# One core, attention and a gated MLP: when the third weight set, a later set's six pieces and the residual x are loaded

## The chip, the cores and the metric

The kernel runs on one core of one Trainium2 chip. The time is that of one execution on the device, in microseconds (us); a result is the median of several runs. A profile is one further execution, recorded instruction by instruction; its span runs from the first to the last instruction on the core.

## The reference

x has 2048 rows of 576. The result is x, plus sliding-window attention (32 heads of 18, window 256) on the normalised x, plus a gated MLP on the normalised x:

```python
def _A_ref(x, wqkv, wo):          # D = 576, H = 32, Dh = 18, W = 256
    qkv = (x @ wqkv).reshape(B, S, 3, H, Dh).transpose(2, 0, 3, 1, 4)
    q, k, v = qkv[0], qkv[1], qkv[2]
    scores = jnp.einsum("bhqd,bhkd->bhqk", q, k) * (Dh ** -0.5)
    mask = (idx[:, None] - idx[None, :] >= 0) & (idx[:, None] - idx[None, :] < W)
    p = _softmax(jnp.where(mask[None, None], scores, -1e9))
    o = jnp.einsum("bhqk,bhkd->bhqd", p, v)
    return o.transpose(0, 2, 1, 3).reshape(B, S, D) @ wo
def _B_ref(x, w1, w3, w2):        # F = 4608
    return (_silu(x @ w1) * (x @ w3)) @ w2
xn = _layernorm(x)
return x + _A_ref(xn, A_wqkv, A_wo) + _B_ref(xn, B_w1, B_w3, B_w2)
```

(The B_x that the inputs hold is not used. Everything is bf16.)

## The kernel before

The program is recorded operation by operation in Python, in the order in which the lines run; `add` notes engine, reads and writes, and `resolve` works out the semaphore waits. So each engine and each DMA queue executes its instructions in the order of the recording, and a DMA that waits holds up every DMA behind it on the same queue. Two queues issue DMAs: SP's, with nearly all of them, and ACT's, with most W2 blocks and some packs.

The 2048 rows go through in four chunks c of 512. A chunk has these stages:

- projection (L437): q, k and v of the chunk from xnT (the normalised x, transposed) and the packed weights wp and wv. In chunk 0 it is part of the start; in the later ones it opens the chunk.
- 36 units u (the loop `for u in range(NF)`): each computes 128 of the 4608 columns of h with 18 matmuls (L664; nine steps n, two matmuls each, on the two halves of the rows of TensorE). Steps 4 to 7 read xnS, a copy of xnT with its two partition halves exchanged. ScalarE takes the tanh (L673), VectorE makes h (L679, L682) into hT. Between the steps stand the score matmuls of the attention (L557) and, three times in a chunk, the P·V matmuls (L614).
- the W2 stage (`p2_list`, `p2_item`): two halves of the output columns, each 9 blocks of W2 by 16 matmuls (L715), and in each half 20 matmuls of the output projection (L721) and four sums with the residual x (L728), each stored by a DMA on SP (L730). `p2_list` numbers its items n from 0: items 0 to 167 are the first half, 168 to 335 the second. The fourth P·V (after item 19) and its transposes lie in here too.

Weights are loaded as they are needed. A set of W1 and W3 columns (w13, one buffer of 128 x 9 x 512) serves four units. It comes in six pieces of 192 KB, each one DMA on SP by `load_part` (L323), always in the order of the sets: set 0 for units 0 to 3 of chunk 0, and so on, nine to a chunk. There are three buffers; set 3 alone goes into a part of hT that is not in use yet. `owed` counts pieces that are due; `owe_part` issues one after steps 3 and 8 of a unit, and the DMA then waits on SP until that matmul is done. So six owed pieces go out over three units. A W2 block (288 KB, four buffers) is loaded by `load_w2` (L350): the first four on SP during units 20 to 26 of chunk 0, all later ones on ACT's queue as soon as the last matmul of the block before in its buffer is done.

The next chunk is prepared meanwhile: its four x tiles come on SP by `load_x` (L299; seven buffers xp), VectorE normalises them (L358 to L370), SP transposes them by DMA (L395) into xnT, and `xn_swap` (L402) makes xnS of it with two DMAs of 256 KB, recorded at an item of the W2 stage. The four tiles of the chunk itself are loaded a second time, for the residual (`xs`).

In chunk 0 the k and q rows are brought into their places by small DMAs from stage (packs, L502): those of groups g 0 and 1 during the projection, the others by `late_spans` at the units listed there, partly on SP, partly on ACT. The packs of the attention's output (L651, `o_pack`) go on SP too. The recording in chunk 0's start is, in the code before:

```python
            if got == ("q", 0):
                load_w13((), 4)
                span_main(0, 2, "act")
                load_w13((), 2)
            elif got == ("q", 2):
                span_last(0, 2)
                for t in (TB, TB + 1):
                    xslot[t] = load_x(t)
```

Set 0 was issued before this; the six pieces here are set 1, and set 2 and set 3 are the twelve pieces that become due at unit 0 (`owed += 12`). From then on a set becomes due after every fourth unit (after unit 15 of chunk 0 none does, since set 3 has freed no buffer of the three); in a later chunk one more becomes due in the projection.

Of the kernel before, what the change touches and what calls it, by code (L numbers as in the profile page):

```python
# [164 lines left out]
def bass_parallel_sum__sliding_block__glu_gated_swiglu__prompt_kernel(  # L165
# [18 lines left out]
    NC = S // CH  # L184
    TB = CH // 128
    G = H // 4
    NF = F // 128
# [10 lines left out]
    with ExitStack() as es:  # L198
# [78 lines left out]
        def job():  # L277
            nonlocal job_ctr
            i = job_ctr % 3
            job_ctr += 1  # L280
            return JOBS[i]
# [13 lines left out]
        def load_x(t, eng="sp"):  # L295
            nonlocal xp_ctr
            s = xp_ctr % NXP
            xp_ctr += 1
            add(eng, lambda e: e.dma_start(xp[s][:], x2[t * 128:(t + 1) * 128, :]), w=[("xp", s)], dma=f"xp{s}")  # L299
            return s  # L300
# [3 lines left out]
        def w13_at(k):  # L304
            if k == 3:
                return NW13, hT[:, 18:27, :]
            s = (k if k < 3 else k - 1) % NW13
            return s, w13[s]

        owed = 0  # L310

        def load_part(after=(), behind=()):

            nonlocal nfill
            if nfill >= 6 * NC * NFC:
                return
            k, i = divmod(nfill, 6)
            s, dst = w13_at(k)
            part, n = divmod(i, 2)
            c0 = (k % NFC) * 512  # L320
            src = (B_w3, B_w1)[n]
            nfill += 1
            add("sp", lambda e: e.dma_start(  # L323
                dst[64 * n:64 * n + 64, 3 * part:3 * part + 3, :],
                src[192 * part:192 * part + 192, c0:c0 + 512].rearrange("(kd p) f -> p kd f", p=64)),
                r=list(behind), after=after, dma=f"w13_{s}_{n}", **{"j" if i else "w": [("w13", s)]})

        def load_w13(behind=(), parts=6):
            for _ in range(parts):
                load_part((), behind)  # L330

        def last_pe():
            return next(o for o in reversed(P.ops) if o.eng == "pe")
# [131 lines left out]
        def proj_end(later=None, late=None):  # L465
            if pend:
                c, what, banks, last = pend.pop()
                proj_part(c, what, banks, 1, last)
                proj_out(c, what, banks, later, late)
                return what  # L470

        def proj_begin(c, what):
            banks = job()
            last = proj_part(c, what, banks, 0)
            got = proj_end()
            pend.append((c, what, banks, last))
            return got
# [256 lines left out]
        xslot = {}  # L734
# [91 lines left out]
        for what in [("q", 0), ("q", 1), ("q", 2), ("q", 3), ("8", 7), None]:  # L826
            got = proj_begin(0, what) if what else proj_end()
# [3 lines that stand above are left out]
                load_w13((), 2)  # L831
            elif got == ("q", 2):
                span_last(0, 2)
                for t in (TB, TB + 1):
                    xslot[t] = load_x(t)

        PV_COST, PV_AFTER = 6.6, 20
        main, rest = span_main, span_last
# [5 lines left out]
        for c in range(NC):  # L844
# [3 lines left out]
            plan = near if c + 1 < NC else {}  # L848
            stat, apply, xt = ({v[k]: i for i, v in plan.items()} for k in range(3))
            loads = {8: (2,), 17: (3,)} if c + 1 < NC else {}  # L850
            total = 9 * NF + len(att) + 3 * PV_COST
            if c:
                total += 9 * sum(COST[kind] for kind, _ in PROJ)
# [59 lines left out]
            for u in range(NF):  # L913
                at_u = u
                if c == 0 and u == 0:
                    owed += 12
                if u in loads:
                    for i in loads[u]:
                        xslot[(c + 1) * TB + i] = load_x((c + 1) * TB + i)
                b0 = jobs[u] = job()  # L920
                for n in range(9):
                    into = nxt - (clock + 9 - n)
                    if done < len(att) and (clock >= nxt or (n == 8 and into < 3 and clock >= soon)):
                        spaced_step()
                    op = unit_pairs(c, u, n, n + 1, b0[0])
                    clock += 1
                    if n in (3, 8):
                        owe_part(op)
                unit_tanh(u, b0[0])
                if u % 4 == 3 and u < NF - 4 and (c or u != 15):  # L930
                    owed += 6
                if next_pv in pv_ready and clock >= pv_ready[next_pv] and next_pv < 3:
                    j = next_pv
                    next_pv += 1
                    banks = job()
                    pv(c, j, banks)
                    clock += PV_COST
                    for g in (2 * j, 2 * j + 1):
                        for s in range(NS):
                            if pt_of[(c, g, s)][0] != "h":  # L940
                                free.append(pt_of[(c, g, s)])
                    later(u, lambda b=banks: (pv_out(b[0], 0), pv_out(b[1], 1), o_scale(0)))
                    later(u + 1, lambda j=j: (o_turn(2 * j, 0), o_turn(2 * j, 1), o_scale(1)))
                    later(u + 2, lambda j=j: o_turn(2 * j + 1, 0))
                    later(u + 3, lambda j=j: (o_turn(2 * j + 1, 1), o_pack(j, "sp")))
                unit_h(u, b0[0])
                for what in side.pop(u, []):
                    what()
                if u in stat:
                    t = (c + 1) * TB + stat[u]  # L950
                    for part in range(2):
                        ln_stats(t, xslot[t], part)
                if u in xt:
                    xn_send((c + 1) * TB + xt[u])
                if u in apply:
                    t = (c + 1) * TB + apply[u]
                    ln_apply(t, xslot[t])
                for span, a, b, n0, n1, eng in late_spans.get(u, []) if c == 0 else []:
                    span(a, b, only=slice(n0, n1), **({"q_eng": eng} if span is main else {"eng": eng}))
                if c == 0 and u in (8, 9, 10, 11):  # L960
                    buf, key = ((wo, "woz"), (oT, "oTz"))[(u - 8) // 2]
                    part = buf[64:128, 4, :] if u % 2 else buf[96:128, 0:4, :]
                    add("dve", lambda e, part=part: e.memset(part.bitcast(dt.float32), 0.0), **{"j" if u % 2 else "w": [key]})
                if c == 0 and u == 13:
                    for t in range(4):
                        rows = A_wo[252 * (t // 2):252 * (t // 2) + 252, :].rearrange("(s p d) f -> p s d f", p=2, d=Dh)[t % 2, :, :, :]
                        add("sp", lambda e, t=t, rows=rows: e.dma_start(wo[0:126, t, :], rows),
                            r=["woz"], dma="wo", **{"j" if t else "w": ["wo"]})
                    add("sp", lambda e: e.dma_start(wo[0:72, 4, :], A_wo[504:576, :]), r=["woz"], j=["wo"], dma="wo")
                if c == 0 and u in (20, 22, 24, 26):  # L970
                    load_w2()
                if u == 29:
                    xs = [load_x(c * TB + tt) for tt in range(TB)]
            assert done == len(att) and next_pv == 3, (done, next_pv)
            ring_of[:] = [*jobs[NF - 2], *jobs[NF - 1]]
# [7 lines left out]
            for n, item in enumerate(p2_list(c)):  # L983
                p2_item(c, item, xs)
                if n == 3:
                    for u in sorted(side):
                        for what in side.pop(u):
                            what()
                elif n == 19:
                    banks = (ring(), ring())  # L990
                    pv(c, 3, banks)
                    pv_out(banks[0], 0)
                    pv_out(banks[1], 1)
                    o_scale(0)
                    o_turn(6, 0)
                    o_turn(6, 1)
                    o_scale(1)
                    o_turn(7, 0)
                    o_turn(7, 1)
                    o_pack(3, "sp")  # L1000
                elif n == 40 and c + 1 < NC:
                    xn_send((c + 1) * TB + 3)
                elif n == 300 and c + 1 < NC:
                    xn_swap(c + 1, ("sp", "sp"))
                elif n in (100, 120) and c + 2 < NC:
                    t = (c + 2) * TB + (n == 120)
                    xslot[t] = load_x(t)

        with nc.Block() as block:
            P.replay(es, block)  # L1010
# [28 lines left out]
```

## Time and profile before

| | |
|---|---|
| time, median of 3 runs | 563.07 us (562.58, 563.07, 564.58) |
| profiled execution | 563.8 us; its span 562.0 us |
| granted clock of TensorE | 1.0 throughout |
| HBM read, written | 71.29 MB, 2.36 MB |
| DMA packets | 126685, 85.83 MB, mean 153 GB/s |

In the profile PE is TensorE's matmuls, PEld its weight loads (beside the matmuls), DVE VectorE, ACT ScalarE, POOL GpSimd; SPq and ACTq are the queues that issue DMAs. A group of instructions goes by its line: L664 the units, L715 the W2 stage, L721 the output projection, L437 the projections. Where the time goes, by stage of chunk 0, from the timeline of TensorE: start and projection to 22.4 us, units to 103.5, W2 stage to 145.3; a later chunk takes 138.1 (145.27 to 283.35). The share of the 16 DMA engines' time that is busy is highest in the first 50 us, where the first sets, wqkv and the packs all go over SP's queue, and around the end of each chunk's units:

```
DMA  9997879887366377588636655859852675470552
```

(one digit for each of 40 slices of the span, in tenths).

### The profile page before, as it was taken

The page shows a single profiled execution, that of the slowest core. Times are in us where ns is not written, and L with a number is a line of the kernel's source. Part 1 is how long each engine was busy: PE and PEld are TensorE (multiplying, and loading weights), DVE is VectorE, ACT ScalarE, POOL GpSimd, SP SyncE. Part 2 cuts the span into 40 slices and gives each one's busy share as a digit, 9 for nine tenths or more (in the row PEclk, how much of TensorE's full clock was granted, in tenths as well). Part 3 has the DMA queues.
Part 4 walks back from the last instruction along what each step waited for, and adds up shares of the span by engine and source line. Part 5 has one row for each costly group of instructions (what it writes and reads, how often), then busy time and mean ns, then how long its engine had stood idle before and what let it go on. Part 6 is the DMA issues. An engine that isn't in the chain of part 4 may idle for free.

```text
span 562.0 us, 15709 instructions
## 1 busy us (share of the span) xinstructions
PE 555.4 (99%) x6765; PEld 343.9 (61%) x6765; DVE 314.9 (56%) x586; ACT 253.0 (45%) x349; POOL 163.3 (29%) x384
## 2 busy tenths in 40 slices
PE   8999999999999999999999999999999999999998
PEld 3545455677676555477767645547776654555776
DVE  7468788810366778861046678884114567767211
ACT  4347766200176766600038676660004766666000
POOL 6413444400033445430003444533000333433000
PEclk9999999999999999999999999999999999999999
DMA  9997879887366377588636655859852675470552
GB/s 245 208 186 170 204 174 176 203 208 187 99 141 135 101 178 144 136 205 203 176 81 139 158 120 131 163 158 201 191 149 64 138 171 127 117 162 12 138 148 64
DMA packets 126685, 85.83 MB, mean 153 GB/s; under 512 B 34024, under 2 KB 124320, under 8 KB 126616
## 3 DMA queue, kind: packets, MB, share of 16 engines
q1 hardware_dynamic: 89076, 63.16, 49.9%
q10 hardware_dynamic: 37540, 21.66, 15.0%
q8 instruction: 53, 0.87, 0.7%
q14 instruction: 16, 0.13, 0.1%
HBM read 71.29 MB, written 2.36 MB: 131 GB/s over the span
## 4 chain that ended last, share of the span: by engine, by line
PE 97%; DMA 2%; DVE 1%; issue 0%; POOL 0%; ACT 0%
PE ps L664 50%; PE ps L715 24%; PE ps L437 9%; PE ps L557 6%; PE ps L614 4%; PE ps L721 3%; DMA w<-in_B_w_dram 1%; DMA xp<-in_A_x_dram 1%; DVE xn L370 0%; DVE stats L358 0%; DVE stats L360 0%; ACT xnT L389 0%; PE ps L382 0%; POOL rstd L364 0%; DVE ofin L728 0%
## 5 line engine op out<-in xcount | busy, mean ns | idle before, releaser
L664 PE MATMUL ps<-xnT,w 64*128 64x512 bf16 x1400 | 181.3, 376 | 1.1 <-issue 1.1
L664 PE MATMUL ps<-xnS,w 64*128 64x512 bf16 x1120 | 154.0, 376 | 0.0
L715 PE MATMUL ps<-w,hT 128*128 128x288 bf16 x1152 | 147.3, 286 | 0.2 <-DMA w<-in_B_w_dram 0.2
L679 DVE SCALAR_TENSOR_TENSOR gs<-th,ps 128x512 bf16<-128x512 bf16 x144 | 98.0, 681 | 78.6 <-ACT th L673 77.5
L566 ACT ACTIVATE pt<-ps 128x1024 bf16<-128x1024 f32 (+1 forms) x112 | 113.1, 1010 | 63.4 <-PE ps L557 63.1
L715 PEld LDWEIGHTS ps<-w,hT 128*128 128x128 bf16 x1152 | 111.9, 98 | 30.8 <-issue 1.7
L664 PEld LDWEIGHTS ps<-xnT,w 64*128 64x128 bf16 x1400 | 70.0, 94 | 59.5 <-issue 1.5
L593 POOL TENSOR_TENSOR pt<-pt,mk 128x128 int32<-128x128 int32 (+1 forms) x199 | 80.4, 425 | 79.4 <-ACT pt L566 79.4
L682 DVE SCALAR_TENSOR_TENSOR hT<-gs,ps 128x512 bf16<-128x512 bf16 x144 | 98.9, 687 | 4.9
L673 ACT ACTIVATE th<-ps 128x512 bf16<-128x512 f32 x144 | 85.5, 593 | 24.0 <-PE ps L664 23.7
L664 PEld LDWEIGHTS ps<-xnS,w 64*128 64x128 bf16 x1120 | 57.2, 94 | 52.4
L728 DVE TENSOR_TENSOR ofin<-ps,xp 128x288 bf16<-128x288 f32 x32 | 14.7, 458 | 120.1 <-PE ps L721 120.1
L450 ACT ACTIVATE stage<-ps 128x512 bf16<-128x512 f32 x16 | 9.6, 597 | 146.0 <-PE ps L437 143.7
L593 POOL TENSOR_TENSOR hT<-hT,mk 128x128 int32<-128x128 int32 (+1 forms) x31 | 12.4, 421 | 171.5 <-ACT hT L566 171.5
L557 PE MATMUL ps<-qv,kv 64*128 64x320 bf16 (+4 forms) x528 | 52.7, 260 | 0.0
L557 PEld LDWEIGHTS ps<-qv,kv 64*128 64x128 bf16 x528 | 27.3, 94 | 25.8 <-ACT pt L566 0.3
L437 PE MATMUL ps<-xnT,wp 64*128 64x512 bf16 (+1 forms) x360 | 38.7, 355 | 0.0
L566 ACT ACTIVATE stage<-ps 128x1024 bf16<-128x1024 f32 x24 | 24.6, 1023 | 12.6 <-PE ps L557 12.6
L636 DVE STREAM_TRANSPOSE od<-oq 128x256 bf16<-128x256 bf16 x64 | 25.8, 428 | 6.3 <-POOL oq L629 6.3
L437 PEld LDWEIGHTS ps<-xnT,wp 64*128 64x128 bf16 x360 | 19.0, 94 | 14.1 <-issue 0.7
L721 PE MATMUL ps<-wo,oT 128*128 128x288 bf16 x160 | 24.8, 286 | 0.0
L593 POOL TENSOR_TENSOR stage<-stage,mk 128x128 int32<-128x128 int32 (+1 forms) x42 | 17.0, 423 | 17.3 <-ACT stage L566 17.2
(58 smaller groups left out, 341.7 us busy)
## 6 DMA issues: line engine op xcount, KB each, us to landing
w<-in_B_w_dram SPq DMA_DIRECT2D x210, 192.0 KB, 4.2
w<-in_B_w_dram ACTq DMA_DIRECT2D x68, 288.0 KB, 3.3
xp<-in_A_x_dram SPq DMA_DIRECT2D x29, 144.0 KB, 4.4
out_dram<-ofin SPq DMA_DIRECT2D x32, 72.0 KB, 1.7
xnS<-xnT SPq DMA_DIRECT2D x8, 256.0 KB, 5.0
oT<-od SPq DMA_DIRECT2D x56, 36.0 KB
pt<-in_A_wqkv_dram SPq DMA_DIRECT2D x4, 288.0 KB, 6.7
hT<-in_B_w_dram SPq DMA_DIRECT2D x6, 192.0 KB, 5.3
```

The lines of the kernel that those rows point to most:

```text
L437: op = add("pe", lambda e, out_=out_, st=st, mv=mv, n=n, r0=r0, first=first: e.matmul(out_, st, mv, start=first, stop=(part == 1 and n == ...
L557: add("pe", lambda e, r0=r0, out_=out_, kb=kb, q0=q0, nb=nb: e.matmul(out_, kb4[r0:r0 + 64, g, kb + NV - NB, :] if kb < 0 else kv[r0:r0 + ...
L566: add("act", lambda e: e.activation(pt_slot(sl)[:, 0:w, :], PS[:, SC[0]:SC[1] + 1, 0:w].rearrange("p r q -> p q r"), ACT.Exp, scale=scale) ...
L593: add("pool", lambda e, vb=vb, mm=mm: e.tensor_tensor(vb, vb, mm, ALU.mult), r=(key if n == 0 else []) + ["mk"], **{"w" if n == 0 else "j" ...
L614: add("pe", lambda e, p=p, q=q, pr=pr, sl=sl, g=g, pos=pos, q0=q0, nb=nb, col=col, first=first, n=n: e.matmul(PS[32 * q:32 * q + VW, banks ...
L636: add("dve", lambda e: e.transpose(od[i][:, g % 2, c0:c0 + CH // 2], oq[:, c0:c0 + CH // 2]), r=["oq", "oq0"], **{"j" if half or g % 2 els ...
L664: op = add("pe", lambda e, n=n, r0=r0, r=r, k=k, src=src: e.matmul(PS[:, b0 + r, :], wt[r0:r0 + 64, k, fl * 128:(fl + 1) * 128], src, star ...
L673: add("act", lambda e: e.activation(th[i][:], PS[:, bg, :], ACT.Tanh, scale=0.5), r=[("ps", bg)], w=[("th", i)])
L679: add("dve", lambda e: e.scalar_tensor_tensor(out=gs[i][:], in0=th[i][:], scalar=1.0, in1=PS[:, bg, :], op0=ALU.add, op1=ALU.mult), r=[("t ...
L682: add("dve", lambda e: e.scalar_tensor_tensor(out=hT[:, u, :], in0=gs[i][:], scalar=0.5, in1=PS[:, bu, :], op0=ALU.mult, op1=ALU.mult), r= ...
L715: add("pe", lambda e: e.matmul(bank, hT[:, f, tt * 128:(tt + 1) * 128], w2[sl][:, k, :], start=(f == 0), stop=False), r=[("h", f), ("w2", ...
L721: add("pe", lambda e: e.matmul(bank, oT[:, k, tt * 128:(tt + 1) * 128], wo[:, k, d0:d0 + HD], start=False, stop=(k == 4)), r=[("oT", j) fo ...
```

## The change

Five edits in the scheduling; no computing instruction changes, and every byte that was loaded is loaded once as before.

- Chunk 0's set 2 is recorded as one run of six pieces right after the packs of groups 0 and 1, where the x tiles 4 and 5 stood. At unit 0 six pieces become due (set 3), not twelve.
- The x tiles 4 to 7 are loaded at units 11, 13, 15 and 17 of chunk 0. Tiles 6 and 7 were at units 8 and 17.
- The set that became due after unit 31 (the second of the next chunk) no longer does; its six pieces are issued in the W2 stage at items 60, 105, 150, 200, 245 and 290, each waiting for the matmul recorded last.
- The residual x tiles are loaded at unit 31, not 29.
- The swap that makes the next chunk's xnS is recorded at item 176, not 300.

```diff
             elif got == ("q", 2):
                 span_last(0, 2)
-                for t in (TB, TB + 1):
-                    xslot[t] = load_x(t)
+                load_w13()
...
             loads = {8: (2,), 17: (3,)} if c + 1 < NC else {}
+            if c == 0:
+                loads = {11: (0,), 13: (1,), 15: (2,), 17: (3,)}
...
                 if c == 0 and u == 0:
-                    owed += 12
+                    owed += 6
...
-                if u % 4 == 3 and u < NF - 4 and (c or u != 15):
+                if u % 4 == 3 and u < NF - 8 and (c or u != 15):
                     owed += 6
...
-                if u == 29:
+                if u == 31:
                     xs = [load_x(c * TB + tt) for tt in range(TB)]
...
-                elif n == 300 and c + 1 < NC:
+                elif n == 176 and c + 1 < NC:
                     xn_swap(c + 1, ("sp", "sp"))
                 elif n in (100, 120) and c + 2 < NC:
                     t = (c + 2) * TB + (n == 120)
                     xslot[t] = load_x(t)
+                elif n in (60, 105, 150, 200, 245, 290) and c + 1 < NC:
+                    load_part((last_pe(),))
```

On TensorE, VectorE, ScalarE and GpSimd the instructions and their order stay the same; only the order of the DMAs on SP changes.

## The prediction

> **What bounds the kernel now.** I read the page first: the share of each engine and the chain of work that ended last.
>
> ```profile
> PE 555.4 (99%) x6765; PEld 343.9 (61%) x6765; DVE 314.9 (56%) x586; ACT 253.0 (45%) x349; POOL 163.3 (29%) x384
> ...
> PE 97%; DMA 2%; DVE 1%; issue 0%; POOL 0%; ACT 0%
> ```
>
> TensorE is busy 555.4 of 562.0 us and holds 97% of the chain. So a change that leaves its instructions as they are can only take away holes in TensorE's stream or make new ones. The waits of PE list all holes:
>
> ```profile
> PE ps L748 <- DVE oq L743: 1.2, 1, 1.2
> PE ps L382 <- DVE xn L370: 1.1, 2, 0.7
> PE ps L664 <- issue: 1.1, 1, 1.1
> PE ps L715 <- DMA w<-in_B_w_dram: 0.2, 1, 0.2
> PE ps L437 <- ACT xnT L389: 0.2, 1, 0.2
> ```
>
> The first, second and last lie before 12.2 us, in the start that the diff does not touch. Two are within its reach: 1.1 at L664 and 0.2 at L715. The timeline of PE shows the first (start, length, engine, line, tiles, count, idle before):
>
> ```profile
> 38.12 0.38 PE L664 MATMUL ps<-xnT,w 64*128 64x512 bf16 x2
> 39.57 1.04 PE L664 MATMUL ps<-xnT,w 64*128 64x512 bf16 x8 [1.06 <-issue]
> ```
>
> The x2 closes unit 7 (its n = 8), the x8 opens unit 8, the first that reads the third weight set, in w13 buffer 2. "issue" means that the profile shows no releaser, so I looked at the queue that loads the set (timeline of SP):
>
> ```profile
> 24.44 0.94 SPq L299 DMA_DIRECT2D xp<-in_A_x_dram  x2
> 25.43 2.78 SPq L323 DMA_DIRECT2D w<-in_B_w_dram  x4
> 28.25 4.66 SPq L502 DMA_DIRECT2D kv<-stage  x3
> 32.95 3.04 SPq L323 DMA_DIRECT2D w<-in_B_w_dram  x2
> 36.03 4.32 SPq L323 DMA_DIRECT2D hT<-in_B_w_dram  x6
> ```
>
> and at the two late pieces alone (L323, issued 32.9 to 36):
>
> ```profile
> L323 SPq DMA_DIRECT2D w<-in_B_w_dram x2: 1466/1496/1527, 33.0 to 34.5; - x2
> ...
>   PEld ps L664: 1.5, 1
> ...
> DMA to landing us min/median/max: 5.0/5.2/5.4
> ```
>
> The last piece goes out at 34.5 and lands 5.0 later, at 39.5; TensorE goes on at 39.57. That hole is the lateness of the third set, which stood behind two x tiles and three packs. The other hole:
>
> ```profile
> 107.06 9.48 PE L715 MATMUL ps<-w,hT 128*128 128x288 bf16 x76
> 116.75 4.58 PE L715 MATMUL ps<-w,hT 128*128 128x288 bf16 x36 [0.21 <-DMA w<-in_B_w_dram]
> ```
>
> A W2 block issued on ACT's queue at 110.69 came late; the chain has 6.00 us of DMA there.
>
> **The change, part by part.** *Third set in one run.* It removes the hole at unit 8. Idle is counted from the end of a matmul, but pairs follow each other every 0.216 us (1.73 for 8 pairs in the chain), so without the wait unit 8 would have begun at 38.12 + 0.216 = 38.34: the loss is 1.23. With the change the six pieces start at 24.44, where the x tiles stood. At 0.70 each (2.78 / 4) the last goes out at about 27.9; the four issued there before took 6.1 to 7.3 us to land, so the set is in by 35.2, 3.1 us before it is read. Gain 1.23.
>
> What is pushed back: four pieces of the fourth set now also precede the packs of g 2 to 4, which move from 28.25 to about 24.44 + 6 x 0.70 + 4 x 0.72 = 31.5 and end near 36.2. Their first reader is the ninth score step, at 51.78. The last two pieces of the fourth set follow by 37.6 and land by 43.6 (6.0, the longest of that set's six); unit 12 needs them at 48.35 - 1.23 = 47.1. The fifth set's last pieces go out near 44.5, before at 51.3 to 52.7; unit 16 reads it at 58.29 - 1.23. The x tiles, now at units 11 and 13 in place of 24.44, go out after 50; DVE first reads one at 71.20 (L358). The moved waits on PE positions name matmuls long done when SP reaches them. All this costs nothing; without that cover each late set would cost about what unit 8 lost.
>
> *Six pieces taken from units 32 to 34 and spread over W2.* Before, they went out from 102.1 to 108.0, beside the first W2 blocks: those issued at 108.7 and 112.7 took 5.3 and 4.9 us, that of 110.69 the 6.00 above. Blocks issued 114.6 to 120.9 took 3.0 to 4.2. A block is wanted three blocks (48 matmuls x 0.1225, 5.88) after its slot came free, about 5.7 after its issue. With the pieces gone, the third block is in time. Last matmul start 116.25, next due 116.38, came at 116.75: gain 0.37. The other chunks show no such hole.
>
> Their new places cost something. Items 60 and 105 go out near 118 to 120, behind the o packs, beside blocks that take 3.0 to 4.2 of 5.7 or more: room 1.5, a piece needs 0.82 (six issued at 158.6 to 162.0 landed after 3.5 to 4.2, so (162.0 + 4.2 - 158.6 - 3.5) / 5). Items 245 and 290 stand beside blocks of 2.9 to 3.4: covered. Items 150 and 200 stand on both sides of the xnS swap, and there is little room:
>
> ```profile
> 126.21 1.19 SPq L402 DMA_DIRECT2D xnS<-xnT  x2
> ```
>
> The swap has the same place: in SP's order it followed the first four stores at once, without a PE wait, so moving it from item 300 to 176 only keeps it ahead of the pieces. But the W2 block issued on ACT right behind it was already nearly late (L350, issued 127.2, and in the third chunk 403.3):
>
> ```profile
> L350 ACTq DMA_DIRECT2D w<-in_B_w_dram x1: 374/374/374, 127.2 to 127.2; - x1
> ...
> DMA to landing us min/median/max: 5.5/5.5/5.5
> ```
>
> ```profile
> L350 ACTq DMA_DIRECT2D w<-in_B_w_dram x1: 375/375/375, 403.3 to 403.3; - x1
> ...
> DMA to landing us min/median/max: 5.6/5.6/5.6
> ```
>
> In the second chunk the same block (265.3) took 4.5. Wanted at 5.68 after issue, less 0.09 between a landing and the matmul (39.48 to 39.57), they have 0.10, -0.02 (call it 0) and 1.10 of room. Item 200 comes at 125.09 + 32 x 0.1225 = 129.0, while the swap still runs (its halves took 4.7 and 5.3 from 126.2 and 126.8). No row has swap, piece and block together, so I bound it: the piece may be served after the block (delay 0), or wholly within its time (0.82); with item 150 having pushed the swap as well, 1.64. With 0 nothing is lost; with 0.82, 0.72 + 0.82 + 0 = 1.54; with 1.64, 1.54 + 1.64 + 0.54 = 3.72. The one comparable row, the swap's own effect, varies by 1.1 us between chunks, so it picks no end; I take half a piece, 0.41: 0.31 + 0.41 + 0 = 0.72. It cannot go below nothing, since the removed pieces never stood beside this block.
>
> The Trainium skill (DMA: Bandwidth & Descriptors, "Queues, rings and completion order") says that each DMA engine takes turns between the queues it has work for, a packet at a time. By that rule SP's piece is served in full while ACT's block is, and the give-back would be that of 0.82, not of 0.41.
>
> *Residual x from unit 29 to 31.* Four issues, now behind four o packs; used only by the first store, some 20 us later. Nothing.
>
> **Sum.** The profiled run took 563.8 (span 562.0 and 1.8 around it): 563.8 - 1.23 - 0.37 + 0.72 = 562.92. It stands 0.73 above the median 563.07, so against the median: 562.19.
>
> **Rivals.**
> 1. *Nothing is given back:* the piece of item 200 waits out the swap on SP's own queue while ACT's block finishes. For it: the block lands only 0.7 after the swap's second half. 563.07 - 1.60 = 561.47.
> 2. *Whole piece inside the block's time:* queues share evenly and the piece is ready 3 us before the block is due. 561.47 + 1.54 = 563.01, no change. The Trainium skill's rule above would bring this one about; the slower block beside the early pieces (5.3 against 3.0) speaks for it, the second chunk's 4.5 beside a swap against so full a price.
> 3. *Slower:* items 150 and 200 both come ahead of the block behind the swap, in all three chunks. It decides against the change once the delay passes 0.85, where the stalls reach 1.60. At 1.64: 561.47 + 3.72 = 565.19. Against it: item 150 goes out near 124, over two us before the swap, when the queues are less full (DMA share 0.80 in 120 to 130).
> 4. *The hole stays or moves to the fourth set:* only if the run of six, with four more behind it, fills the queue so that landings stretch from 7.3 to over 10. 562.19 + 1.23 = 563.42.
>
> **How the numbers follow.** Forecast (part of a piece, 561.7 to 562.7) 0.42; rival 1, 0.30; rival 2, 0.15; rival 3, 0.08; rival 4, 0.05. Time 562.2. The range of 8 in 10 takes in rivals 1 and 2 with some 0.3 of spread between measurements: 561.2 to 563.3. About 0.5%, 2.8 us, is what a measurement of this kernel can tell from no change. Every case above lies within it; faster by so much would need 2.8 us of holes where 1.6 are within reach (0.03), slower needs rival 3 at nearly twice its bound or a new hole in each chunk (0.04), so within 0.5%: 0.93.
>
> **What will show it.** Right: no hole before unit 8; six pieces in a row from about 24.4 on SP; PE 1.2 us earlier from there; no hole at L715 near 115; at most small holes at L715 near 131.5 and 407, released by a W2 block that took 5.7 to 6.3. Wrong: a hole at unit 8 or 12; blocks behind the swap still at 5.5 or less (rival 1), or over 6.5 (rival 3); a DMA wait anywhere at L437 or L557.

## The result and the profile after

The change makes the kernel slower: 565.77 us median (565.05 to 566.75, five runs) against 563.07 (562.58 to 564.58) before, a ratio of 1.0048 with an interval of 1.0034 to 1.0063. The forecast was 562.2, with a range to 563.3. Run once more later (below), the change took 566.07.

The page after: engines, chain, and the waits of PE.

```profile
PE 557.4 (99%) x6765; PEld 344.1 (61%) x6765; DVE 314.6 (56%) x586; ACT 253.0 (45%) x349; POOL 163.2 (29%) x384
...
PE 96%; DMA 3%; DVE 0%; POOL 0%; ACT 0%; issue 0%
```

```profile
PE ps L715 <- DMA w<-in_B_w_dram: 1.7, 3, 0.9
PE ps L748 <- DVE oq L743: 1.2, 1, 1.2
PE ps L382 <- DVE xn L370: 0.6, 1, 0.6
PE ps L437 <- ACT xnT L389: 0.2, 1, 0.2
```

The wait at L664 is gone, as forecast. In its place L715 waits three times for W2 blocks, 1.7 us, where it waited once for 0.2. The first part is plain in the queue and in the units (timeline of SP; the six pieces of the run alone; timeline of PE, where this profile's unit 0 begins at 23.41):

```profile
24.50 4.94 SPq L323 DMA_DIRECT2D w<-in_B_w_dram  x6
29.48 2.58 SPq L323 DMA_DIRECT2D hT<-in_B_w_dram  x4
32.11 3.30 SPq L502 DMA_DIRECT2D kv<-stage  x3
```

```profile
L323 SPq DMA_DIRECT2D w<-in_B_w_dram x6: 612/704/1201, 24.5 to 28.8; - x6
...
DMA to landing us min/median/max: 4.5/4.8/5.0
```

```profile
39.17 1.24 PE L664 MATMUL ps<-xnT,w 64*128 64x512 bf16 x10
40.25 0.35 PE L557 MATMUL ps<-qv,kv 64*128 64x320 bf16 x4
40.44 1.03 PE L664 MATMUL ps<-xnS,w 64*128 64x512 bf16 x8
```

The last piece goes out at 28.8 and is in by 33.8; the x10 at 39.17 holds the end of unit 7 and the first steps of unit 8, with nothing between. The new holes, in the timeline of PE:

```profile
132.82 1.40 PE L715 MATMUL ps<-w,hT 128*128 128x288 bf16 x10 [0.35 <-DMA w<-in_B_w_dram]
```

```profile
269.67 2.13 PE L715 MATMUL ps<-w,hT 128*128 128x288 bf16 x16 [0.40 <-DMA w<-in_B_w_dram]
272.74 3.48 PE L715 MATMUL ps<-w,hT 128*128 128x288 bf16 x27 [0.94 <-DMA w<-in_B_w_dram]
```

They stand in the second half of the W2 stages of chunks 0 and 1, behind the swap. The prediction had looked for small ones near 131.5 and 407; the two in chunk 1 came where it expected none. Chunk 1's queue on SP, before and then after, shows what is new ahead of them:

```profile
256.23 1.06 SPq L299 DMA_DIRECT2D xp<-in_A_x_dram  x2
260.55 3.64 SPq L730 DMA_DIRECT2D out_dram<-ofin  x4
264.29 1.18 SPq L402 DMA_DIRECT2D xnS<-xnT  x2
```

```profile
256.28 0.69 SPq L323 DMA_DIRECT2D w<-in_B_w_dram  x1
257.02 0.60 SPq L299 DMA_DIRECT2D xp<-in_A_x_dram  x1
257.67 0.65 SPq L323 DMA_DIRECT2D w<-in_B_w_dram  x1
258.37 0.59 SPq L299 DMA_DIRECT2D xp<-in_A_x_dram  x1
260.60 1.44 SPq L730 DMA_DIRECT2D out_dram<-ofin  x2
262.09 0.60 SPq L323 DMA_DIRECT2D w<-in_B_w_dram  x1
262.81 1.43 SPq L730 DMA_DIRECT2D out_dram<-ofin  x2
264.35 1.17 SPq L402 DMA_DIRECT2D xnS<-xnT  x2
267.46 13.31 SPq L323 DMA_DIRECT2D w<-in_B_w_dram  x3
```

The first two pieces (items 60 and 105) go out with the two x tiles, before the stores. What they do can be read from the four stores behind them, which are small: before, and after,

```profile
L730 SPq DMA_DIRECT2D out_dram<-ofin x4: 332/334/343, 260.5 to 263.9; - x4
...
DMA to landing us min/median/max: 1.6/2.1/3.0
```

```profile
L730 SPq DMA_DIRECT2D out_dram<-ofin x4: 333/342/528, 260.6 to 263.9; - x4
...
DMA to landing us min/median/max: 5.1/5.9/6.5
```

A store that landed after 2.1 us takes 5.9: when the swap is issued, transfers issued earlier are still waiting to be served, a backlog. The W2 block behind the swap, before and after, takes 7.3 us in place of 4.5:

```profile
L350 ACTq DMA_DIRECT2D w<-in_B_w_dram x1: 375/375/375, 265.3 to 265.3; - x1
...
DMA to landing us min/median/max: 4.5/4.5/4.5
```

```profile
L350 ACTq DMA_DIRECT2D w<-in_B_w_dram x1: 374/374/374, 265.4 to 265.4; - x1
...
  PE ps L715: 0.9, 1
...
DMA to landing us min/median/max: 7.3/7.3/7.3
```

It is the block that the hole of 0.94 waits for. The busy share of the DMA engines says the same (windows: busy time of PE, PEld, DVE, ACT, POOL, clock, DMA share, GB/s), before and after:

```profile
256.00:264.00 8.00, 8.00 (x67) 6.40 (x66) 1.83 (x4) 0.00 (x0) 0.00 (x0) 1.00 0.79 200
264.00:272.00 8.00, 8.00 (x68) 6.37 (x67) 0.00 (x0) 0.00 (x0) 0.00 (x0) 1.00 0.89 221
```

```profile
256.50:265.50 9.00, 9.00 (x76) 7.20 (x74) 1.83 (x4) 0.00 (x0) 0.00 (x0) 1.00 1.05 246
265.50:273.50 8.00, 6.66 (x54) 4.87 (x53) 0.00 (x0) 0.00 (x0) 0.00 (x0) 1.00 1.04 247
```

From 0.79 and 0.89 the share rises to 1.05 and 1.04: the engines are busy throughout. A high share for a while is not enough for a hole, though: without the pieces of items 150 and 200 (below) the share is 1.08 in 256 to 266, but 0.74 in 266 to 274, and chunk 1 has no hole; the change has 1.03 in both.

TensorE's instructions are the same in all kernels here, two more fillers at the start of three of them aside (fillers are matmuls in the idle time of the start whose result is not used). So a profile can be cut into stages by the first matmul of each: start of unit 0, units of chunk 0 (to the first L715), W2 stages of chunks 0, 1 and 2 (to the first L437 of the next chunk). All else, the later units (82.6 to 83.1), the projections (13.61) and the last W2 stage (41.76), hardly differs. The kernels below the second row are those of the next section.

| profile | unit 0 at | units, chunk 0 | W2 c0 | W2 c1 | W2 c2 | median us | ratio to before, interval |
|---|---|---|---|---|---|---|---|
| before | 22.36 | 81.16 | 41.75 | 41.69 | 41.69 | 563.07 | |
| the change | 23.41 | 79.87 | 41.90 | 43.38 | 41.89 | 565.77 | 1.0048 (1.0034, 1.0063) |
| early edits only | 23.59 | 79.87 | 41.44 | 41.69 | 41.78 | 562.65 | 0.9992 (0.9983, 1.0000) |
| late edits only | 22.42 | 81.04 | 41.70 | 43.90 | 42.31 | 567.01 | 1.0059 (1.0048, 1.0070) |
| no 60, 105 | 23.45 | 79.87 | 41.96 | 41.82 | 42.80 | 564.17 | 1.0014 (1.0005, 1.0023) |
| no 150, 200 | 22.66 | 79.87 | 41.37 | 41.69 | 42.11 | 562.69 | 0.9989 (0.9981, 0.9998) |
| pieces late | 22.42 | 79.86 | 41.37 | 41.69 | 41.92 | 562.35 | 0.9987 (0.9978, 0.9996) |
| pieces and swap late | 22.24 | 79.86 | 41.37 | 41.69 | 41.69 | 563.39 | 0.9994 (0.9984, 1.0004) |
| pieces and swap late, again | 22.74 | 79.88 | 41.37 | 41.69 | 41.69 | 562.45 | 0.9986 (0.9977, 0.9995) |
| x tiles late | 22.47 | 79.87 | 41.78 | 41.69 | 42.92 | 564.43 | 1.0019 (1.0008, 1.0030) |
| pieces and swap late, 12 fillers | 22.39 | 79.86 | 41.37 | 41.69 | 41.69 | 562.32 | 0.9978 (0.9969, 0.9987) |
| before, 12 fillers | 22.36 | 80.48 | 41.51 | 41.69 | 42.19 | 563.03 | 0.9994 (0.9985, 1.0004) |
| change, 12 fillers | 22.64 | 79.86 | 42.49 | 43.41 | 43.13 | 566.53 | 1.0050 (1.0035, 1.0066) |
| change again | 22.51 | 79.86 | 42.39 | 43.51 | 42.04 | 566.07 | 1.0054 (1.0037, 1.0071) |

The kernel before had a median of 563.20 to 563.43 in the later groups of runs. A W2 stage without a hole takes 41.37 in chunk 0 and 41.69 in chunks 1 and 2, 124.75 together. The change is at 127.17, 127.94 and 129.03 in its three profiles (the one with 12 fillers included): 2.4 to 4.3 us of loss. Before is at 125.13, and at 125.39 with 12 fillers.

### The profile page after: what moved, and what is told of

Read it like the earlier page. It is cut to its first block, busy times and chain, and to the rows that moved or that the text cites. A ratio compares the mean times of both kernels' runs of the same rounds, so it can differ in the third digit from the quotient of the medians.

```text
span 564.1 us, 15709 instructions
## 1 busy us (share of the span) xinstructions
PE 557.4 (99%) x6765; PEld 344.1 (61%) x6765; DVE 314.6 (56%) x586; ACT 253.0 (45%) x349; POOL 163.2 (29%) x384
## 4 chain that ended last, share of the span: by engine, by line
PE 96%; DMA 3%; DVE 0%; POOL 0%; ACT 0%; issue 0%
PE ps L664 50%; PE ps L715 23%; PE ps L437 10%; PE ps L557 6%; PE ps L614 3%; PE ps L721 3%; DMA w<-in_B_w_dram 2%; DMA xp<-in_A_x_dram 0%; PE ps L748 0%; PE ps L382 0%; ACT xnT L389 0%; DVE xn L370 0%; POOL rstd L364 0%; DVE stats L358 0%; DVE ofin L728 0%
## 5 line engine op out<-in xcount | busy, mean ns | idle before, releaser
L664 PE MATMUL ps<-xnT,w 64*128 64x512 bf16 x1400 | 181.1, 376 | 0.0
L664 PE MATMUL ps<-xnS,w 64*128 64x512 bf16 x1120 | 154.0, 376 | 0.0
L715 PE MATMUL ps<-w,hT 128*128 128x288 bf16 x1152 | 147.8, 286 | 1.7 <-DMA w<-in_B_w_dram 1.7
L715 PEld LDWEIGHTS ps<-w,hT 128*128 128x128 bf16 x1152 | 111.7, 98 | 33.0 <-DMA w<-in_B_w_dram 2.9
L664 PEld LDWEIGHTS ps<-xnT,w 64*128 64x128 bf16 x1400 | 70.2, 94 | 58.2 <-issue 0.2
L664 PEld LDWEIGHTS ps<-xnS,w 64*128 64x128 bf16 x1120 | 57.2, 94 | 52.3
L437 PE MATMUL ps<-xnT,wp 64*128 64x512 bf16 (+1 forms) x360 | 38.7, 355 | 0.0
L437 PEld LDWEIGHTS ps<-xnT,wp 64*128 64x128 bf16 x360 | 19.1, 94 | 14.0 <-issue 0.7
L437 PE MATMUL ps<-wv,xnT 64*128 64x288 bf16 x288 | 22.5, 290 | 0.3 <-ACT xnT L389 0.2
```

Source lines behind the costliest of these rows:

```text
L437: op = add("pe", lambda e, out_=out_, st=st, mv=mv, n=n, r0=r0, first=first: e.matmul(out_, st, mv, start=first, stop=(part == 1 and n == ...
L664: op = add("pe", lambda e, n=n, r0=r0, r=r, k=k, src=src: e.matmul(PS[:, b0 + r, :], wt[r0:r0 + 64, k, fl * 128:(fl + 1) * 128], src, star ...
L715: add("pe", lambda e: e.matmul(bank, hT[:, f, tt * 128:(tt + 1) * 128], w2[sl][:, k, :], start=(f == 0), stop=False), r=[("h", f), ("w2", ...
```

## The experiments

**The two halves of the change.** Early edits only: the late ones are undone.

```diff
-                if u % 4 == 3 and u < NF - 8 and (c or u != 15):
+                if u % 4 == 3 and u < NF - 4 and (c or u != 15):
...
-                if u == 31:
+                if u == 29:
...
-                elif n == 176 and c + 1 < NC:
+                elif n == 300 and c + 1 < NC:
...
-                elif n in (60, 105, 150, 200, 245, 290) and c + 1 < NC:
-                    load_part((last_pe(),))
```

> Only the early edits: set 2 of chunk 0 in one run, six pieces due at unit 0, x tiles 4 to 7 at units 11 to 17; the W2 stage, the residual x and the swap as before. Theory (the time is lost in the W2 stage, where the four pieces of items 60 to 200 fill the DMA queues beside the swap; the early part is worth its 1.23): no hole before unit 8, a hole of 0.2 to 0.6 at L715 near 115 as before, about 561.8 us. Rival A (the early run itself costs time, by a later set or a slower start): 563 or more, and a hole or a later unit 0 in every profile. The start of unit 0 is 22.36 in the profile of before and 23.41 in that of the change with the same instructions ahead of it: if that is chance, this profile shows either of the two.

Measured: units of chunk 0 in 79.87, no hole at unit 8; 562.65 against 563.41, 0.76 less, at the edge of what can be told, and above the 561.8 expected. The early run is not shown to cost anything, so Rival A falls; its late unit 0 is not in every profile with the early edits (22.42 with the pieces late). The hole near 115 was not there in this profile (W2 of chunk 0: 41.44), though the six pieces stood where they had been: it comes and goes. Unit 0 began at 23.59, late as in the change.

Late edits only: the early ones are undone.

```diff
-                load_w13()
+                for t in (TB, TB + 1):
+                    xslot[t] = load_x(t)
...
-            if c == 0:
-                loads = {11: (0,), 13: (1,), 15: (2,), 17: (3,)}
...
-                    owed += 6
+                    owed += 12
```

> Only the late edits: the six pieces at items 60 to 290, swap at item 176, residual x at unit 31; chunk 0's start as before. Theory: the hole of 1.06 before unit 8 is back, holes at L715 near 133, 270 and 411 of 2.3 us in all, 563.07 - 0.37 + 2.35, about 565.0 us; with the start 1.05 later by chance up to 566. Rival A (the early run costs): under 564.

Measured: 567.01, above the 566 expected at most and slower than the change itself; the hole at unit 8 is back (0.90), and the W2 stages stand 3.2 above 124.75. The whole loss is in the late edits, and the early gain goes against it.

**Which pieces.** The change without the pieces of items 60 and 105, and then without those of 150 and 200:

```diff
-                elif n in (60, 105, 150, 200, 245, 290) and c + 1 < NC:
+                elif n in (150, 200, 245, 260, 275, 290) and c + 1 < NC:
```

> The change with the pieces of items 60 and 105 moved to 260 and 275; 150 and 200 stay. Theory (a backlog from all four): the blocks behind the swap take about 1 us less than the 6.2 to 7.3 of the change, holes under 1 us in all, 561.7 to 562.8 us. Rival B (the prediction's picture: only the pieces on both sides of the swap count): the holes stay at 2 us or more, 563.5 to 564.5 us.

```diff
-                elif n in (60, 105, 150, 200, 245, 290) and c + 1 < NC:
+                elif n in (60, 105, 245, 260, 275, 290) and c + 1 < NC:
```

> The change with the pieces of items 150 and 200 moved to 260 and 275; 60 and 105 stay. Theory (a backlog from all four): the blocks behind the swap take 5.3 to 6 us, holes under 1 us in all, 561.6 to 562.6 us. Rival B (only 150 and 200 count): no hole at all, 561.5 us, and blocks behind the swap at 4.5 to 5.6 as in before.

Measured: 564.17 without 60 and 105, 562.69 without 150 and 200. Against the kernel before in the same group of runs that is 0.8 above and 0.7 below, where the change stood 2.7 above. So both pairs matter, 150 and 200 more. The theory missed the first: it said holes under 1 us and at most 562.8, but the stages kept 0.6, 0.1 and 1.1 us, and 564.17 lies in the range that was given to Rival B. The blocks behind the swap tell how the pairs act. Without 60 and 105 (chunk 2's, then chunk 1's):

```profile
L350 ACTq DMA_DIRECT2D w<-in_B_w_dram x1: 374/374/374, 403.4 to 403.4; - x1
...
DMA to landing us min/median/max: 6.7/6.7/6.7
```

```profile
L350 ACTq DMA_DIRECT2D w<-in_B_w_dram x1: 375/375/375, 265.3 to 265.3; - x1
...
DMA to landing us min/median/max: 4.6/4.6/4.6
```

and without 150 and 200, chunk 1's:

```profile
L350 ACTq DMA_DIRECT2D w<-in_B_w_dram x1: 374/374/374, 264.0 to 264.0; - x1
...
DMA to landing us min/median/max: 5.5/5.5/5.5
```

Chunk 1's block took 4.5 before. The pieces at 150 and 200 alone add 0.1, those at 60 and 105 alone 1.0, all four 2.8: more than the two parts together, as a backlog would have it. Chunks 0 and 2 read otherwise. There the block took 5.5 and 5.6 before, 6.2 and 5.8 in the change; with 150 and 200 alone it takes 6.2 and 6.7, with 60 and 105 alone 5.0 and 6.0. So in these two chunks 150 and 200 alone bring losses (0.6 and 1.1) as large as the change's first profile has (0.5 and 0.2), and 60 and 105 alone none and 0.4. That is nearer to Rival B's picture, on one profile each.

**What stands with them.** The change with the two x tiles of the W2 stage moved behind the swap; the pieces stay.

```diff
-                elif n in (100, 120) and c + 2 < NC:
-                    t = (c + 2) * TB + (n == 120)
+                elif n in (255, 280) and c + 2 < NC:
+                    t = (c + 2) * TB + (n == 280)
```

> The change with the two x tiles of items 100 and 120 moved to items 255 and 280; pieces as in the change. These tiles exist in the W2 stages of chunks 0 and 1 only. Theory (backlog of everything on SP before the swap): chunk 1's W2 stage, 43.4 in the change, comes down to 41.8 to 42.4, chunk 0's by up to 0.3, chunk 2's stays at 41.9 to 42.3; 563.5 to 564.8 us. Rival B (only 150 and 200 count): no change, 565.5 us.

Measured: chunk 1's W2 stage falls from 43.38 to 41.69, all of its loss, though no piece was moved; its block behind the swap takes 4.7 us again. Chunk 2, where no x tiles stand, keeps a hole (42.92, above the 42.3 expected and more than in the change's first profile). So in chunk 1 the pieces cost what they do because two x tiles (288 KB) go out among them. Rival B, that only 150 and 200 count, falls with this for chunk 1, not for the other two. Two x tiles go out among the pieces of chunk 0 as well, and moving them brought its stage only from 41.90 to 41.78; why chunk 1 suffers most stays open.

**Out of the way.** All six pieces behind the swap; the first goes out with the last W2 block that the stage itself needs:

```diff
-                elif n in (60, 105, 150, 200, 245, 290) and c + 1 < NC:
+                elif n in (245, 254, 263, 272, 281, 290) and c + 1 < NC:
```

> The change with all six pieces at items 245 to 290, every ninth item, so none before or beside the swap. Theory (backlog of pieces, x tiles, stores and swap in the DMA queues up to block 31): every hole of the W2 stages goes, the blocks behind the swap take 4.5 to 5.7 as in before, the unit stage of chunk 0 keeps its gain: 563.4 - 1.6 = 561.8 us, ratio 0.997. Rival C (the loss belongs to the swap's new item or to residual x at unit 31, not to the pieces): 564 us or more.

Measured: 562.35, ratio 0.9987, not quite the 0.997 expected; no hole, and only chunk 2 is 0.2 above its stage without holes. The swap at item 176 and the residual x at unit 31 are in this kernel too, so Rival C falls. And with the swap back at item 300, where the pieces before it now hold it:

```diff
-                elif n == 176 and c + 1 < NC:
+                elif n == 300 and c + 1 < NC:
...
-                elif n in (60, 105, 150, 200, 245, 290) and c + 1 < NC:
+                elif n in (245, 254, 263, 272, 281, 290) and c + 1 < NC:
```

> As the run before, and the swap recorded at item 300 again, which is now behind pieces that wait for items up to 290, so that it starts some 14 us later than in before, after the blocks that matter. Theory: the blocks behind the swap's old place take 3.0 to 4.3, no hole; no faster than the run before where that has none, so 561.5 to 561.8 us, and with less spread between runs; xnS lands near 146 and is read near 158. Rival D (a later swap delays the next chunk's first unit): a hole before unit 0 of chunks 1 to 3.

The swap goes out 37.2 us after the stage's first matmul, in before 22.7 us (timeline of SP of this kernel):

```profile
120.67 3.64 SPq L730 DMA_DIRECT2D out_dram<-ofin  x4
133.03 6.11 SPq L323 DMA_DIRECT2D w<-in_B_w_dram  x6
139.25 1.18 SPq L402 DMA_DIRECT2D xnS<-xnT  x2
```

The three W2 stages are at 41.37, 41.69 and 41.69, without a hole, and no hole stands before the next chunk's unit 0 (Rival D falls). The blocks issued where the swap had stood took 3.3, 3.0 and 3.3 us, against 5.5, 4.7 and 5.9 with the swap there and all else the same. The time, 563.39, was above what that says, with runs from 561.95 to 565.15. So the kernel was measured once with two more fillers, and once more as it is.

> As the run with the late swap, and twelve matmuls in place of ten in the first idle-time filler of the start (its result is not used). The start of unit 0 was 22.4 or 23.4 to 23.6 in profiles of kernels with the same instructions up to there. If a pause of TensorE before its full speed is what puts the start late, unit 0 begins at 22.3 to 22.8 each time and the median falls by about 0.4 us against the run before; if it is chance independent of the pause, no difference.

> The kernel with late pieces and late swap once more, ten fillers. Its runs lay in two groups before, 562.0 to 562.5 and 563.0 to 565.2, while those with twelve fillers lay between 562.0 and 562.7. If the fillers make that difference, the median is again near 563.4 and the spread over 1.5 us; if the first time was chance, the median is 562.2 to 562.6, like that with twelve.

The edit of the first of the two, beside those above:

```diff
-        warm(4, 10)
+        warm(4, 12)
```

With twelve fillers: 562.32 (562.02 to 562.68), ratio 0.9978, faster than before and than the change. With ten again: 562.45 (562.13 to 563.43). So the first 563.39 was for the greater part chance, and the fillers, which do nothing for the output, are not shown to help. It also says how far medians can be trusted: the same kernel came out 0.94 apart, so differences of under a us, such as the late swap's from the kernel with only the pieces late (562.35), are read from the profiles and not from the times. The waits of PE with twelve fillers:

```profile
PE ps L748 <- DVE oq L743: 1.2, 1, 1.2
PE ps L437 <- ACT xnT L389: 0.2, 1, 0.2
```

**The chance of the start taken out.** Both kernels with twelve fillers, and the change again:

> The kernel before with twelve fillers in place of ten at the start. Unit 0 at 22.3 to 22.5, holes at unit 8 (1.06) and at L715 (0.2) as before. If the start alone makes part of before's runs about 1 us longer, its median falls by 0.3 to 0.6 to about 562.9 us and the runs lie closer together; if the start does not matter, 563.4.

> The change with the same twelve fillers: its difference to the run before is the change without the chance of the start. Theory (all that is lost is lost in the W2 stages, 2.4 us of holes against 1.6 won): 0.7 to 1.5 above the run before, 563.6 to 564.4 us. Rival E (something outside the W2 stages costs as well, which one profile does not show): over 564.9.

> The change once more, unaltered, for a second profile and more times. Theory: 564.3 to 565.8 us, W2 stages of 41.7 to 42.2, 42.5 to 43.9 and 41.8 to 42.9, unit 0 at 22.4 or 23.4. If the loss of 2.7 us measured at first was partly chance, the median lies nearer 564.5.

Measured: 563.03, 566.53 and 566.07. The fillers change neither kernel beyond its interval. The difference of the first two, 3.5 us, is above what was expected and in the range given to Rival E, but the profile of that kernel puts it in the W2 stages: 42.49, 43.41 and 43.13, 4.3 above 124.75, with units of 79.86 and nothing new elsewhere. The change again, 566.07, lies a little above the 565.8 expected at most. The loss is larger and varies more from one execution to the next than the change's first profile let one think, chunk 2's from 0.2 to 1.4. The loss was not chance.

## Why the prediction was wrong, step by step

- *Third set in one run, gain 1.23:* right in mechanism and size in the profile (units of chunk 0 from 81.16 to 79.87, 1.29). In the times it is worth less, 0.76; the hole differs between executions (1.06, 0.90, 0.39 in the three profiles that have it).
- *The packs, x tiles and later sets pushed back cost nothing:* right; no profile has a hole in the units of chunk 0 from them.
- *Hole near 115, gain 0.37:* right, but it is not in every execution, as the early edits alone show; and before with 12 fillers has such a hole in chunk 2 (0.32), where the prediction saw none.
- *"Items 60 and 105 ... room 1.5, a piece needs 0.82" and so nothing lost:* this step failed. Each piece was held against the room of one block at its side. But pieces, x tiles, stores and swap follow each other on SP within ten us, and what is not served at once stands ahead of what comes later. The busy shares shown then, 0.80 in 120 to 130, left at most a fifth, 2 us, of room for four pieces of 0.82. In chunk 1 taking away any one part, 60 and 105, 150 and 200 or the x tiles, brings the stage to within 0.13 of one without holes, so it is their sum, carried along as a backlog, that makes them.
- *"They have 0.10, 0 and 1.10 of room":* the second chunk was counted as safe because its block had taken 4.5. Its loss was the largest, 1.7 to 1.8 in the change's three profiles, for the same reason: the room was measured without the backlog.
- *Half a piece, 0.41, as the delay:* mis-sized. The delays measured behind the swap are 0.7, 2.8 and 0.2 in the change's own profile, and up to 1.2, 2.9 and 1.5 in its two others; the sum of the give-back is 2.4 to 4.3 where 0.72 was taken and 3.72 was the far end. In chunks 0 and 2 the mechanism was that of the prediction, items 150 and 200 beside the swap, and the size was off.
- *Rival 3* was the case that came, with a cause wider than its own words: 60 and 105 belong to it. That its price lies so near (565.19 against 565.77) is luck: it had 1.54, 0.54 and 1.64 us for the three chunks, the change's first profile has 0.53, 1.69 and 0.20, and a late start of unit 0 adds 1.05. Its chance was 0.08, and the range ended at 563.3, though the prediction's own bound on the unknown delay, 1.64, led past it.
- The Trainium skill's rule on turns between queues (DMA: Bandwidth & Descriptors, "Queues, rings and completion order") agrees with what the traces show: SP's pieces make ACT's blocks late, from 4.5 to 7.3 us in chunk 1, although the queues are separate. No run here shows the turns themselves. The prediction applied it to one piece only.
- *Moving the swap and the residual x costs nothing:* right as far as can be told, by the kernel with late pieces, which has both.

The change's first profile is 2.0 us longer than before's, in these parts: 1.05 the start, -1.29 the units of chunk 0, +0.15, +1.69 and +0.20 the W2 stages, +0.15 chunk 1's units, the rest about 0.1 in all. The start is not the change's: kernels with the same instructions up to there had unit 0 at times from 22.24 to 23.59, the change itself at 23.41 and 22.51.

## What to carry to other kernels

Before a transfer is moved into a stage, add up all bytes that the shared DMA engines must move there, in both queues and in order, and not only the transfer against its neighbour. Here a busy share of 0.79 and then 0.89 still left the blocks in time; 1.05 and then 1.04 made one 2.8 us late. In a stage whose blocks are just in time, the place that worked for extra loads was beside and behind the last block that the stage itself needs, here items 245 and later; with the swap there too, three profiles show no hole in any W2 stage. Where a bound on an unknown delay reaches past the gain, the range has to reach there as well.

## What was not expected of the hardware

Transfers became later by far more than the rate rose: a 288 KB block lands after 3.0 us with nothing else near it, 4.5 to 5.6 beside the swap and 7.3 with pieces and x tiles around the swap, and the stores went from 2.1 to 5.9, while the rate rose only from 221 to 247 GB/s.

In executions of the same start TensorE is fast from different times on: the first ten fillers took 4.45 us in both, the three at 6.6 us 0.82 in before and 1.46 in the change, and unit 0 came at 22.36 and 23.41. The granted clock on record is 1.00 in both, so only the lengths show it. The Trainium skill (TensorE: Matmul & The Clock Gate, "Part 1: The HAM clock gate (the "warmup" mystery)") has a free-running window for it, so that the moment varies between runs; the profiles agree, with 1.35 us between the earliest and the latest unit 0. Whether more fillers narrow it stays open: the three profiles with twelve lie between 22.36 and 22.64.
